# Batch 0 of an attention and gated-MLP kernel: q's product in 64-column tiles, one-pass transposes, twelve unread matmuls left out, another order of all work

## The chip, the cores and the metric

The kernel runs on one core of a Trainium2 chip. The time is device microseconds (us) of one execution. The core has a matrix engine (TensorE, PE in the rows; PEld is its loading of weights), a vector engine (VectorE, DVE), a scalar engine (ScalarE, ACT), GpSimd (POOL), and SyncE (SP), which here issues the DMAs. PE writes to PSUM, which POOL can't reach.

## What is computed

First a linear-time attention with product features, for 4 batches and 4 heads of 32 columns over 1088 positions; then a gated MLP whose gate mixes the positions with a 1088 x 1088 matrix. The reference, cut to that:

```python
def phi(x):
    a = np.einsum('rd,bhsd->bhsr', S1, x)
    b = np.einsum('rd,bhsd->bhsr', S2, x)
    return np.einsum('bhsi,bhsj->bhsij', a, b).reshape(*x.shape[:-1], r * r)   # r = 8
q_p, k_p = phi(q), phi(k)
kv = np.einsum('bhsf,bhsd->bhfd', k_p, v)
z = np.sum(k_p, axis=2)
x = np.einsum('bhsf,bhfd->bhsd', q_p, kv) / (np.einsum('bhsf,bhf->bhs', q_p, z)[..., None] + 1e-06)
...                                            # heads side by side: x is (4, 1088, 128)
h = gelu_tanh(x @ w_in)                        # w_in 128 x 1024
u, v = h[..., :512], h[..., 512:]
v_n = (v - mean(v)) / np.sqrt(var(v) + 1e-06) * g_ln
v_s = np.einsum('ts,bsd->btd', w_sg, v_n) + b_sg[None, :, None]   # w_sg 1088 x 1088
out = x + (u * v_s) @ w_out                    # w_out 512 x 128
```

## The kernel before

Large products are done in fp32r with operands that are split into a high and a low part (names with `_h` and `_l`): high x high, low x high and high x low are added in PSUM. Small products in the head are plain fp32, for which the trace shows two records each. Positions lie in 9 blocks of 128. PSUM has eight banks: `pst` (three, handed out in turn, `ps` in the rows), `pzt` (two, `pz`) and `pot` (three, `po`).

Batch 0's head goes like this. `k1_0` (L531) makes k's factors, `features` (L270) on DVE their products, `k2_0` (L539) the key product in 64-column weight tiles; `kv_0` (L551, L553) cuts it into `kvx`, a block-diagonal operand with a column for the denominator. `q2_0` (L608) makes q's factors in three blocks of 384 positions, ACT copies one of two (L622), DVE multiplies (L623). `q3_0` (L586) is q's product with `kvx`: for each block of 384 positions six matmuls with 128 weight columns and 66 moving ones. `xt_0` (L593 to L595) divides by the denominator on DVE, `tr_0` (L602) transposes with a matmul by the identity, ACT and DVE split x into its two parts (L630, L631). Then the nine gate groups `v1_0` (L636 to L638; 512 columns, one for each block of positions) make v; ACT does the GELU (L653), and batch-norm statistics follow on DVE (L642) or ACT (L655, L656). The norm is done in three groups of blocks (2, 4 and 3 of them) by small operations on DVE or POOL (L299 to L333), then v is scaled (L336, L669) and split into `ar` and `rs` (L676, L677). The mixing product of batch 0 comes next, w's blocks by v's: `z0` (L700, L702, L698 for w's low part) into `po`, and a second one (L1264, L1266, L1262) into `pz`. Beside it the attention of batch 1 begins: `k1` (L947), q's factors (L980), the key product (again L539).

w_in, w_out and S1, S2 come as 64-bit floats and are split by a chain of integer operations on DVE and ACT, `split64` (L473 to L496; its last step L496 makes the low part, `win_l`). w itself is cast to its high part by ACT (L671); the low part `w_l` is made by POOL for the first seven blocks (L718) in pieces of 420, 420 and 248 columns, and by DVE for the last two. Batches 1 to 3 follow with the same kinds of operations (L849 to L851 for most of the mixing).

Every operation is a step of a list with an engine, its dependences and its buffers (`step`, `add`). A table of numbers, `ORDER`, says in which order the steps are recorded; each engine runs its own in that order, and SP issues its DMAs in it. A step that waits holds back all that stands behind it on its engine. The list has also `KEEP = 12` steps `keep`, which multiply a part of `win_h` by another into the first `pz` bank, and which nothing reads. In the head, the DMAs' places in the table were bound by a rule: `first_loads` gives an order, and each load had to come behind the one before it in its row.

Of the kernel before, what the change touches and what calls it, by code (L numbers as in the profile page):

```python
# [34 lines left out]
KEEP = 12  # L35
# [173 lines left out]
def tile_kernel(ctx: ExitStack, tc: tile.TileContext, qd, kd, vd, sd, wd, bd, wind, gd, woutd, identd, outd):  # L209
# [290 lines left out]
    for n, dma, f in first_loads():  # L500
# [3 lines left out]
        if n == "win1":  # L504
            split64("s", None, None, raw_s, 16, s_f, ["s"], ())
            split64("wi1", win_h[:, DG:], win_l[:, DG:], lambda: raw_w("wi1"), DG, None, ["win1"], ())
# [73 lines left out]
    def view(c):  # L580
        return pzt[c % 2][:, : 6 * n2].rearrange("p (g e) -> p g e", e=D + 1)
# [801 lines left out]
```

## Time and profile before

| | us |
|---|---|
| runs: median of 3 (lowest to highest) | 327.1 (326.97 to 327.31) |
| the profiled execution, whole | 327.88 |
| its span, first to last instruction | 326.1 |
| PE busy | 316.9 (97%) |
| DVE busy | 257.4 (79%) |
| ACT busy | 208.5 (64%) |
| POOL busy | 49.8 (15%) |

Rows of the profile give the start of an instruction or of a run of equal ones in us from the span's start, or sums over a group. Matmuls are pipelined, so their records overlap, and what one costs in a row of them is the distance between starts. `[... <-DVE x L1]` behind an instruction means that its engine was idle before it, until that instruction on DVE was done. A chain follows what ended last back to the start, each piece with its length.

### The profile page before, as it was taken

The page shows a single profiled execution, that of the slowest core. Times are in us where ns is not written, and L with a number is a line of the kernel's source. Part 1 is how long each engine was busy: PE and PEld are TensorE (multiplying, and loading weights), DVE is VectorE, ACT ScalarE, POOL GpSimd, SP SyncE. Part 2 cuts the span into 40 slices and gives each one's busy share as a digit, 9 for nine tenths or more (in the row PEclk, how much of TensorE's full clock was granted, in tenths as well). Part 3 has the DMA queues.
Part 4 walks back from the last instruction along what each step waited for, and adds up shares of the span by engine and source line. Part 5 has one row for each costly group of instructions (what it writes and reads, how often), then busy time and mean ns, then how long its engine had stood idle before and what let it go on. Part 6 is the DMA issues. An engine that isn't in the chain of part 4 may idle for free.

```text
span 326.1 us, 6435 instructions
## 1 busy us (share of the span) xinstructions
PE 316.9 (97%) x2303; PEld 287.2 (88%) x2303; DVE 257.4 (79%) x567; ACT 208.5 (64%) x494; POOL 49.8 (15%) x125
## 2 busy tenths in 40 slices
PE   8997999999999999999999999999999999999995
PEld 6764789888888998799899999898999999999994
DVE  4799889999987888787866788996864794878564
ACT  5577795557887993565889855457869952333241
POOL 0197673100004300000005200000013200000000
PEclk9999999999999999999999999999999999999999
DMA  7992875657778857972285239940553035506602
GB/s 222 362 384 68 292 222 173 185 156 155 222 216 264 267 160 222 298 266 61 82 286 171 72 99 251 295 108 3 158 150 143 1 106 178 182 26 210 215 2 69
DMA packets 42128, 57.10 MB, mean 175 GB/s; under 512 B 4208, under 2 KB 37104, under 8 KB 42096
## 3 DMA queue, kind: packets, MB, share of 16 engines
q1 hardware_dynamic: 41952, 56.62, 56.2%
q8 instruction: 18, 0.29, 0.4%
q14 instruction: 14, 0.11, 0.1%
q10 hardware_dynamic: 144, 0.06, 0.1%
HBM read 46.73 MB, written 9.95 MB: 174 GB/s over the span
## 4 chain that ended last, share of the span: by engine, by line
PE 77%; DVE 8%; ACT 7%; DMA 4%; issue 2%; SPq 1%; DVEq 0%; ACTq 0%
PE pz L849 14%; PE pz L850 13%; PE pz L851 13%; PE ps L764 2%; PE pz L860 2%; PE po L801 2%; PE ps L766 2%; PE ps L539 2%; PE ps L765 2%; PE ps L1007 2%; PE po L803 2%; PE po L802 2%; PE pz L861 2%; PE ps L1041 2%; PE po L700 2%
## 5 line engine op out<-in xcount | busy, mean ns | idle before, releaser
L849 PE MATMUL pz<-w_h,ar 128*128 128x420 f32 (+1 forms) x288 | 94.2, 327 | 0.2 <-DVE gt L780 0.2
L850 PE MATMUL pz<-w_h,ar 128*128 128x420 f32 (+1 forms) x288 | 93.2, 324 | 0.0
L851 PE MATMUL pz<-w_l,ar 128*128 128x420 f32 (+1 forms) x288 | 93.1, 323 | 0.0
L849 PEld LDWEIGHTS pz<-w_h,ar 128*128 128x128 f32 x288 | 54.1, 188 | 4.3 <-issue 1.7
L850 PEld LDWEIGHTS pz<-w_h,ar 128*128 128x128 f32 x288 | 54.1, 188 | 1.3 <-DVE ar L825 0.2
L851 PEld LDWEIGHTS pz<-w_l,ar 128*128 128x128 f32 x288 | 54.2, 188 | 0.6
L824 ACT CAST ar<-vn 128x512 fp32r<-128x512 f32 x40 | 24.5, 618 | 27.1 <-PE pz L851 20.2
L795 ACT CAST gh<-gt 128x420 fp32r<-128x420 f32 (+1 forms) x47 | 23.0, 493 | 21.2 <-DVE gt L794 18.5
L770 ACT ACTIVATE u<-ps 128x420 f32<-128x420 f32 (+1 forms) x48 | 22.4, 470 | 13.5 <-PE ps L766 7.3
L825 DVE TENSOR_TENSOR ar<-vn,ar 128x512 fp32r<-128x512 f32 x40 | 27.1, 684 | 3.4 <-ACT ar L824 3.2
L796 DVE TENSOR_TENSOR gl<-gt,gh 128x420 fp32r<-128x420 f32 (+1 forms) x47 | 24.6, 533 | 5.6 <-ACT gh L795 5.4
L794 DVE TENSOR_TENSOR gt<-gt,u 128x420 f32<-128x420 f32 (+1 forms) x47 | 24.9, 532 | 3.6 <-ACT u L770 2.9
L336 ACT ACTIVATE vn<-vn,st 128x512 f32<-128x512 f32 x33 | 25.6, 811 | 0.0
L718 POOL TENSOR_TENSOR w_l<-w_f,w_h 128x420 fp32r<-128x420 f32 (+1 forms) x21 | 22.3, 1085 | 18.5 <-DVE sp_wi_t L474 14.3
L780 DVE SCALAR_TENSOR_TENSOR gt<-pz,g_col,b_bc 128x420 f32<-128x420 f32 (+1 forms) x31 | 17.6, 569 | 3.9 <-PE pz L861 2.8
L1050 ACT ACTIVATE vn<-ps 128x512 f32<-128x512 f32 x27 | 16.0, 593 | 6.0 <-PE ps L1043 6.0
L1053 ACT ACTIVATE kp<-vn,st 128x512 bf16<-128x512 f32 x27 | 19.4, 720 | 0.5
L319 POOL TENSOR_TENSOR st<-st 128x4 f32<-128x4 f32 (+2 forms) x8 | 3.0, 381 | 103.3 <-DVE st L301 103.3
L764 PE MATMUL ps<-x_h,win_h 128*128 128x420 f32 (+1 forms) x48 | 15.8, 330 | 0.2 <-ACT r L1016 0.2
L766 PE MATMUL ps<-x_l,win_h 128*128 128x420 f32 (+1 forms) x48 | 15.7, 328 | 0.0
L765 PE MATMUL ps<-x_h,win_l 128*128 128x420 f32 (+1 forms) x48 | 15.7, 327 | 0.0
L801 PE MATMUL po<-gh,wout_h 128*128 128x420 f32 (+1 forms) x47 | 15.7, 334 | 0.0
(264 smaller groups left out, 722.5 us busy)
## 6 DMA issues: line engine op xcount, KB each, us to landing
w_h<-td SPq DMA_DIRECT2D x26, 420.0 KB
w_l<-td SPq DMA_DIRECT2D x52, 210.0 KB
td<-tmp SPq DMA_DIRECT2D x16, 315.0 KB
w_f<-in_w SPq DMA_DIRECT2D x9, 544.0 KB
eb<-dq SPq DMA_DIRECT2D x6, 364.0 KB
ea<-dq SPq DMA_DIRECT2D x12, 182.0 KB
vn<-in_k SPq DMA_DIRECT2D x3, 576.0 KB
tmp<-in_w SPq DMA_DIRECT2D x8, 210.0 KB
```

The source lines that it names most:

```text
L336: return A.activation(self.vn(t), self.vn(t), AF.Identity, bias=self.nm[:, t : t + 1], scale=self.rs[:, t : t + 1])
L718: return G.tensor_sub(w_l[t][:, cs], w_f[t][:, cs], f32(w_h[:, t, cs]))
L764: mm(o, lhsT=win_h[:, ws], rhs=xh[:, cs], start=True, stop=False)
L770: add("A", 0.02 + ap(cw), lambda: A.activation(utt[plan.got[u]][:, :cw], ps(k)[:, :cw], AF.Gelu_apprx_tanh), r=[k], take={u: "u"}, free=[k ...
L794: add("V", dv(cw), lambda: V.tensor_mul(gt(k)[:, :cw], gt(k)[:, :cw], utt[plan.got[u]][:, :cw]), r=[u], w=[k], free=[u], port=1)
L795: add("A", ac(cw), lambda: A.copy(ght[plan.got[h]][:, :cw], gt(k)[:, :cw]), r=[k], take={h: "gh"})
L796: add("V", dv(cw), lambda: V.tensor_sub(glt[plan.got[l]][:, :cw], gt(k)[:, :cw], f32(ght[plan.got[h]][:, :cw])), r=[h, k], take={l: "gl"}, ...
L824: add("A", ac(n), lambda: A.copy(dst[:, 0], q()), r=r, w=[key])
L825: add("V", dv(n), lambda: V.tensor_sub(dst[:, 1], q(), f32(dst[:, 0])), r=r, w=[key], port=1)
L849: mm(o, lhsT=ar[e][:, 0, t], rhs=wh, start=first, stop=False, skip_group_check=True)
L850: mm(o, lhsT=ar[e][:, 1, t], rhs=wh, start=False, stop=False, skip_group_check=True)
L851: mm(o, lhsT=ar[e][:, 0, t], rhs=wl, start=False, stop=last, skip_group_check=True)
```

## The change

Six things are changed. `q3_0` makes 12 matmuls with 64 weight columns for a block of 384 positions, in place of six with 128, and lays the result out so that the two denominators of a pair of heads stand side by side. The addition of 1e-6 to the denominator goes from DVE to a new ACT step, `xd`. `kv_0` makes `kvx` with two DVE operations in place of four. `tr_0` uses PE's transpose mode, which takes one pass in place of fp32's two records. The 12 `keep` steps are gone. The low part of w_in's second half, `win_l`, is added up by POOL (`G`) and not by DVE. The loads of the head may stand anywhere in `ORDER`, and the whole table is another one, so that steps of all batches stand in other places.

```diff
-KEEP = 12
...
-    1, 11, 12, 13, 14, 15, 16, 17, 18, 42, 49, 2, 3, 4, 46, 47, 48, 0, 52, 43,
+    2, 1, 11, 12, 3, 4, 13, 14, 0, 15, 16, 17, 18, 50, 42, 45, 46, 43, 53, 47,
...
-        row = "w" if n[1:].isdigit() and n[0] == "w" else "raw" if n in ("win0", "win1", "wout") else n if n in "gb" else ""
-        step(("ld", n), "SP", 0.47 * len(dma), f, dma=dma, order=[last[x] for x in {row, ""} if x in last], after=[("wi1", 5), ("wi1", 4)] if n == "wout" else [])
-        ids[n] = last[row] = ids["ld", n]
+        step(("ld", n), "SP", 0.47 * len(dma), f, dma=dma, after=[("wi1", 5), ("wi1", 4)] if n == "wout" else [])
+        ids[n] = ids["ld", n]
...
-            split64("wi1", win_h[:, DG:], win_l[:, DG:], lambda: raw_w("wi1"), DG, None, ["win1"], ())
+            split64("wi1", win_h[:, DG:], win_l[:, DG:], lambda: raw_w("wi1"), DG, None, ["win1"], (), G)
...
     def kv_0():
-        a = pzt[1][:, :P].rearrange("p (a d) -> p a d", a=4)
-        m = mask.rearrange("p (h d) -> p h d", h=2)
+        m = mask.rearrange("p (h d) -> p h d", h=2)[:, :, :1].broadcast_to([P, 2, D + 1])
         for i in range(2):
-            V.tensor_mul(kvx()[:, i, :, :D], a[:, 3 * i].unsqueeze(1).broadcast_to([P, 2, D]), m)
-        for i in range(2):
-            V.tensor_mul(kvx()[:, i, :, D], a[:, i + 1, :1].broadcast_to([P, 2]), m[:, :, 0])
+            a = pzt[1][:, (3 * D - 1) * i :][:, : D + 1]
+            V.tensor_mul(kvx()[:, i], a.unsqueeze(1).broadcast_to([P, 2, D + 1]), m)
...
     def q3_0(c):
         for t in range(3):
             for p in range(2):
-                mm(
-                    pzt[c % 2][:, 2 * n2 * t : 2 * n2 * (t + 1)].rearrange("q (h p e) -> q p h e", h=2, p=2)[:, p],
-                    lhsT=qp0(c, p)[:, P * t : P * t + P], rhs=kvx()[:, p], start=True, stop=True,
-                )
+                o = view(c)[:, 2 * t : 2 * t + 2, (D + 1) * p :][:, :, : D + 1]
+                for e in (0, 64):
+                    mm(o[e : e + 64], lhsT=qp0(c, p)[:, P * t + e : P * t + e + 64], rhs=kvx()[:, p], start=True, stop=True)
+
+    den0 = staged("den", [P, 12], None)
+
+    def xd_0(c):
+        return A.activation(den0(c).rearrange("p (g e) -> p g e", e=2), view(c)[:, :, D : D + 2], AF.Identity, bias=eps_t)
 
     def xt_0(c):
-        den = stage([P, 12], f"den{c}", f"den0_{c}")
-        V.tensor_scalar(den, view(c)[:, :, D], EPS, None, op0=ALU.add)
-        V.reciprocal(den, den)
+        V.reciprocal(den0(c), den0(c))
...
     def tr_0(c):
         for t in range(3):
             cs = slice(P * t, P * t + P)
-            mm(ps(("px0", c))[:, cs], lhsT=xt0[c][:, cs], rhs=ident(), start=True, stop=True)
+            mm(ps(("px0", c))[:, cs], lhsT=xt0[c][:, cs], rhs=ident(), start=t == 0, stop=t == 2, is_transpose=True, skip_group_check=True)
...
-    for i in range(KEEP):
-        step(("keep", i), "PE", 0.233, lambda: mm(pzt[0], lhsT=win_h[:, DG : DG + P], rhs=win_h[:, DG:], start=True, stop=True), [("wi1", "hi")], w=[("psn", 0)])
```

What the new table does to the engines' order is seen in three places. The line numbers below are each kernel's own; in the new kernel they are two to five lower.

The first is DVE behind the features of k, up to the first product of the attention (`r`). L623 (new L620) multiplies q's factors, `sp_wi` are steps of the split of w_in's second half, `den` are denominators. Before:

```order
L623 TENSOR_TENSOR vn<-pz_114,eb 128x384
L623 TENSOR_TENSOR vn<-po_117,ea 128x384
L551 TENSOR_TENSOR sg_kvx<-pz_115,mask 128x2x32 x2
L553 TENSOR_TENSOR sg_kvx<-pz_115,mask 128x2 x2
L623 TENSOR_TENSOR vn<-po_117,eb 128x384
L623 TENSOR_TENSOR vn<-ps_111,ea 128x384
L473 TENSOR_SCALAR sp_wi_t<-sg_wraw_wi_277 128x512
L593 TENSOR_SCALAR den_0_314<-pz_114 128x12
L594 RECIPROCAL den_0_314<-den_0_314 128x12
L595 TENSOR_TENSOR r_101<-pz_114,den_0_314 128x384
```

And now:

```order
L620 TENSOR_TENSOR vn<-po_117,ea 128x384
L620 TENSOR_TENSOR vn<-pz_114,eb 128x384
L471 TENSOR_SCALAR sp_wi_t<-sg_wraw_wi_227 128x512
L472 SCALAR_TENSOR_TENSOR sp_wi_t<-sg_wraw_wi_227,sp_wi_t 128x512
L474 SCALAR_TENSOR_TENSOR sp_wi_t<-sp_wi_m,sp_wi_t 128x512
L477 TENSOR_SCALAR sp_wi_g<-sp_wi_t 128x512
L547 TENSOR_TENSOR sg_kvx<-pz_115,mask 128x66 x2
L620 TENSOR_TENSOR vn<-ps_113,ea 128x384
L620 TENSOR_TENSOR vn<-po_117,eb 128x384
L493 TENSOR_TENSOR sp_wi_t<-sp_wi_t,win_h 128x512
L590 RECIPROCAL sg_den_313<-sg_den_313 128x12
L591 TENSOR_TENSOR r_101<-pz_114,sg_den_313 128x384
```

Four steps of the split went ahead of `kvx`, and a fifth ahead of the first reciprocal.

The second is POOL from its first low part of w on; `w_l_321` (new `w_l_315`) is block 0 of it, `w_l_363` (new `w_l_421`) block 1. Before:

```order
L718 TENSOR_TENSOR w_l_321<-w_f_140,w_h 128x420 x2
L930 MEMSET eb 128x64
L718 TENSOR_TENSOR w_l_321<-w_f_140,w_h 128x248
L718 TENSOR_TENSOR w_l_363<-w_f_141,w_h 128x420 x2
L718 TENSOR_TENSOR w_l_363<-w_f_141,w_h 128x248
```

And now:

```order
L713 TENSOR_TENSOR w_l_315<-w_f_140,w_h 128x420 x2
L713 TENSOR_TENSOR w_l_315<-w_f_140,w_h 128x248
L494 TENSOR_TENSOR win_l<-sp_wi_t,sp_wi_e 128x512
L713 TENSOR_TENSOR w_l_421<-w_f_141,w_h 128x420 x2
L713 TENSOR_TENSOR w_l_421<-w_f_141,w_h 128x248
```

`win_l` came in behind block 0.

The third is PE from the last gate group to the first matmuls of the mixing product; L712 are the `keep` steps, L947 (new L942) and L980 (new L975) belong to batch 1. Before:

```order
L638 MATMUL ps_112<-win_h,x_l 128x512
L712 MATMUL pz_114<-win_h 128x512
L947 MATMUL ps_113<-sk,vn 64x64 x2
L947 MATMUL ps_112<-sk,vn 64x64 x2
L712 MATMUL pz_114<-win_h 128x512 x4
L947 MATMUL ps_111<-sk,vn 64x64 x2
L712 MATMUL pz_114<-win_h 128x512 x4
L947 MATMUL ps_112<-sk,vn 64x64 x2
L947 MATMUL ps_113<-sk,vn 64x64 x2
L700 MATMUL po_116<-w_h,ar_89 128x420
```

And now:

```order
L636 MATMUL ps_111<-win_h,x_l 128x512
L975 MATMUL ps_113<-qld,sk 64x182 x2
L942 MATMUL ps_112<-sk,vn 64x64 x2
L942 MATMUL ps_111<-sk,vn 64x64 x2
L942 MATMUL ps_113<-sk,vn 64x64 x2
L942 MATMUL ps_112<-sk,vn 64x64 x2
L942 MATMUL ps_111<-sk,vn 64x64 x2
L942 MATMUL ps_113<-sk,vn 64x64 x2
L698 MATMUL po_117<-w_h,ar_89 128x420
```

The `keep` steps are out, and batch 1's first matmuls, of which some stood between the gate groups, now all stand behind the last one.

## Rows read from the trace of the kernel before

**Rows 1.** Windows: stretch, length, busy PE, PEld, DVE, ACT, POOL, clock, DMA, GB/s.

```profile
core 0 of [0], span 326.1 us
...
7.00:8.00 1.00, 1.00 (x20) 0.52 (x16) 0.70 (x3) 0.81 (x2) 0.00 (x0) 1.00 1.09 371
...
150.00:200.00 50.00, 50.00 (x409) 46.17 (x408) 36.88 (x79) 36.90 (x92) 6.72 (x24) 1.00 0.45 141
```

**Rows 2.** The chain that ended last, in the head: start, length, what.

```profile
3.05 5.23 DMA sg_vx<-in_v
...
8.32 2.20 PE pz L539 x68
...
16.61 1.01 ACT w_h L671
...
21.30 0.61 ACT vn L653
...
33.81 1.13 PE pz L712 x4
34.94 0.27 PE ps L947 x4
...
36.71 0.39 PE po L700
```

**Rows 3.** PE's weight loads in order of time: start, length, what, count.

```profile
11.94 1.42 PEld L586 LDWEIGHTS pz<-sg_kvx,vn 128*128 128x128 f32 x12 [0.54 <-issue]
...
16.60 1.41 PEld L602 LDWEIGHTS ps<-sg_ident,r 128*128 128x128 f32 x12 [0.55 <-DMA qld<-in_q]
```

**Rows 4.** PE's matmuls in order of time, at the start of the mixing products.

```profile
36.64 0.46 PE L700 MATMUL po<-w_h,ar 128*128 128x420 f32 x1
36.94 0.35 PE L702 MATMUL po<-w_h,ar 128*128 128x420 f32 x1
...
43.28 0.35 PE L1264 MATMUL pz<-w_h,ar 128*128 128x420 f32 x1
```

**Rows 5.** DVE in order of time, in the head.

```profile
17.61 0.55 DVE L623 TENSOR_TENSOR vn<-pz,ea 128x384 f32<-128x384 f32 x1
18.07 0.68 DVE L495 TENSOR_TENSOR sp_wi_t<-sp_wi_t,win_h 128x512 f32<-128x512 f32 x1
18.67 0.68 DVE L480 SCALAR_TENSOR_TENSOR sp_wi_e<-sp_wi_e,sp_wi_g 128x512 f32<-128x512 f32 x1
...
21.05 0.23 DVE L594 RECIPROCAL den<-den 128x12 f32<-128x12 f32 x1
21.32 0.56 DVE L595 TENSOR_TENSOR ea<-pz,den 128x384 f32<-128x384 f32 x1
21.93 0.69 DVE L642 BATCH_NORM_STATS2 st<-vn 128x6 f32<-128x512 f32 x1
...
22.76 0.66 DVE L642 BATCH_NORM_STATS2 st<-vn 128x6 f32<-128x512 f32 x1
...
26.00 1.05 DVE L306 TENSOR_TENSOR st<-st 128x2 f32<-128x2 f32 x1
27.09 0.16 DVE L307 TENSOR_TENSOR st<-st 128x2 f32<-128x2 f32 x1
...
34.95 0.42 DVE L677 TENSOR_TENSOR ar<-vn,ar 128x256 fp32r<-128x256 f32 x1
```

**Rows 6.** The instructions on `win_l`: line, engine, count, ns min/median/max, starts.

```profile
L496 POOL TENSOR_TENSOR win_l<-sp_wi_t,sp_wi_e x1: 1294/1294/1294, 59.5 to 59.5; 128x512 fp32r<-128x512 f32 x1
```

**Rows 7.** POOL in order of time; the second row has pieces of 420 and 248.

```profile
15.30 2.87 POOL L718 TENSOR_TENSOR w_l<-w_f,w_h 128x420 fp32r<-128x420 f32 x2 [14.34 <-DVE sp_wi_t L474]
...
18.83 8.21 POOL L718 TENSOR_TENSOR w_l<-w_f,w_h 128x248 fp32r<-128x248 f32 x8 [0.57 <-DVE sp_wi_t L495]
```

**Rows 8.** Windows, two of PE's emptiest: columns as in rows 1.

```profile
27.00:28.00 1.00, 0.57 (x9) 0.37 (x8) 0.83 (x6) 0.57 (x3) 0.04 (x1) 1.00 0.01 2
...
325.00:326.10 1.10, 0.00 (x0) 0.00 (x0) 0.00 (x0) 0.00 (x0) 0.00 (x0) 0.51 0.00 0
```

**Rows 9.** Groups by line: busy us, mean ns of one, idle before.

```profile
L780 DVE SCALAR_TENSOR_TENSOR gt<-pz,g_col,b_bc 128x420 f32<-128x420 f32 (+1 forms) x31 | 17.6, 569 | 3.9 <-PE pz L861 2.8
```

More of the change, by code (lines that the diff above doesn't have):

```diff
@@ L498, in tile_kernel @@
     step("vx1", "G", 0.1, lambda: G.memset(vx()[:, NT], 1.0))
-    last = {}
     for n, dma, f in first_loads():
-        row = "w" if n[1:].isdigit() and n[0] == "w" else "raw" if n in ("win0", "win1", "wout") else n if n in "gb" else ""
-        step(("ld", n), "SP", 0.47 * len(dma), f, dma=dma, order=[last[x] for x in {row, ""} if x in last], after=[("wi1", 5), ("wi1", 4)] if n == "wout" else [])
-        ids[n] = last[row] = ids["ld", n]
+        step(("ld", n), "SP", 0.47 * len(dma), f, dma=dma, after=[("wi1", 5), ("wi1", 4)] if n == "wout" else [])
+        ids[n] = ids["ld", n]
         if n == "win1":
             split64("s", None, None, raw_s, 16, s_f, ["s"], ())
-            split64("wi1", win_h[:, DG:], win_l[:, DG:], lambda: raw_w("wi1"), DG, None, ["win1"], ())
+            split64("wi1", win_h[:, DG:], win_l[:, DG:], lambda: raw_w("wi1"), DG, None, ["win1"], (), G)
     m4 = mask4.rearrange("q (p h) -> q p h", p=2)
@@ L560, in tile_kernel @@
             ps(("pk0", c))[:, : 3 * 64].rearrange("q (t p x c) -> q t p x c", t=3, p=2, x=2)[:, :, :, 1],
-        ), [pk])
+        ), [pk], r=[pk])
         for i in range(3):
@@ L565, in tile_kernel @@
             step(("kp0", t), "V", 0.34, lambda c=c, i=i, t=t: features(vn[:, t, 512:768], ps(("pk0", c))[:, 64 * i : 64 * i + 64], kb0(c)[:, i]),
-               [("kb0", c)], w=kk, free=[pk] if i == 2 else [])
+               [("kb0", c)], r=[pk], w=kk, free=[pk] if i == 2 else [])
             step(("k2_0", t), "PE", 0.45, lambda t=t: k2_0(t), ["v0", "v1", "vx1"], r=kk + [("vx", 0), ("vx", 1)], w=[("psn", 1)])
     QT = [(("po", 0), ("po", 1)), (("po", 2), ("psn", 0)), None, (("po", 0), ("po", 1)), (("po", 2), ("psn", 0)), None]
-    n2 = 2 * (D + 1)
+    n2 = 2 * (D + 2)
     def pab0(j, i):
@@ L580, in view @@
     def view(c):
-        return pzt[c % 2][:, : 6 * n2].rearrange("p (g e) -> p g e", e=D + 1)
+        return pzt[c % 2][:, : 6 * n2].rearrange("p (g e) -> p g e", e=n2)
     def q3_0(c):
@@ L585, in q3_0 @@
             for p in range(2):
-                mm(
-                    pzt[c % 2][:, 2 * n2 * t : 2 * n2 * (t + 1)].rearrange("q (h p e) -> q p h e", h=2, p=2)[:, p],
-                    lhsT=qp0(c, p)[:, P * t : P * t + P], rhs=kvx()[:, p], start=True, stop=True,
-                )
+                o = view(c)[:, 2 * t : 2 * t + 2, (D + 1) * p :][:, :, : D + 1]
[4 more added lines that the diff above has]
+        return A.activation(den0(c).rearrange("p (g e) -> p g e", e=2), view(c)[:, :, D : D + 2], AF.Identity, bias=eps_t)
     def xt_0(c):
-        den = stage([P, 12], f"den{c}", f"den0_{c}")
-        V.tensor_scalar(den, view(c)[:, :, D], EPS, None, op0=ALU.add)
-        V.reciprocal(den, den)
+        V.reciprocal(den0(c), den0(c))
         V.tensor_tensor(
-            xt0[c].rearrange("p (g d) -> p g d", d=D), view(c)[:, :, :D], den.unsqueeze(2).broadcast_to([P, 12, D]), op=ALU.mult
+            xt0[c].rearrange("p (g e d) -> p g e d", e=2, d=D), view(c).rearrange("p g (e d) -> p g e d", e=2)[:, :, :, :D],
+            den0(c).rearrange("p (g e) -> p g e", e=2).unsqueeze(3).broadcast_to([P, 6, 2, D]), op=ALU.mult
         )
@@ L627, in tile_kernel @@
         step(("q3_0", c), "PE", 1.36, lambda c=c: q3_0(c), ["kv0", ("qp", 2 * c), ("qp", 2 * c + 1)], w=[("psn", c % 2)])
-        step(("xt", c), "V", 0.94, lambda c=c: xt_0(c), [("q3_0", c)] + [("qp", 4)] * (c == 2), r=[("psn", c % 2), "ea"])
+        step(("xd", c), "A", 0.2, lambda c=c: xd_0(c), [("q3_0", c)], r=[("psn", c % 2)])
+        step(("xt", c), "V", 0.8, lambda c=c: xt_0(c), [("q3_0", c), ("xd", c)] + [("qp", 4)] * (c == 2), r=[("psn", c % 2), "ea"])
         step(("tr", c), "PE", 0.68, lambda c=c: tr_0(c), [("xt", c), "ident"], r=["ea"], take={("px0", c): "ps"})
```

185 rows, old and new, of the table ORDER are left out of this document.

## The prediction

> **What bounds the kernel now.** I read the windows first, then the chain of waits, then each engine's timeline for the first 45 us. In the windows TensorE (PE) is busy 50.00 of the 50 us from 150 to 200, and it is nearly like that from 42 to 322 us [rows 1]: there the end is PE's work added up. The head is different. Its chain goes from v's load, which lands at 8.3, over the key product L539 to the first GELU at 21.30; at 33.81 it rests on four L712, matmuls whose result nobody reads, and at 36.71 it comes to the first mixing matmul of batch 0, L700 [rows 2]. PE does fillers there because it has nothing else that it may do. So PE time that is taken out counts only as far as the work that PE waits for comes earlier too, and I cost the change twice: by PE's work, and by when that chain lets PE go.
>
> **PE's work.** The 12 fillers L712 fall away. Four of them stand on the chain with 1.13 us [rows 2], 0.28 each: 12 x 0.28 = 3.4 us. q's product L586 has two records for each fp32 matmul; 12 of them, one third of the batch, take 1.42 us [rows 3], 0.118 apart. It becomes 24 records a third with 64 weight columns. The nearest row is L539, the same width with 64 moving columns for 66: 68 records in 2.20 us, 0.032 apart [rows 2]. 24 x 0.032 = 0.78, so 0.64 is saved in each third, 1.9 in all. At the other bound 64-column weights would keep the old spacing, cost 2.8 a third and lose 4.2 in all; I take the row of the same shape. The nine transposes L602 take 18 records, 12 of them 1.41 us [rows 3]; with one pass each, 9 remain. A one-pass transpose is in no row. Its bounds are a 64-column record's 0.032 and both old records' 0.235; I take 0.118, since one pass is what one record is, and save 9 x 0.118 = 1.1 (1.8 or nothing at the bounds). Together PE loses 3.4 + 1.9 + 1.1 = 6.4 us. Against it stand some two more switches between 64- and 128-column weights: behind such a switch L700 starts at 36.64 and the next matmul 0.30 later instead of 0.19 [rows 4], so 0.2 us for two, which I leave in the range.
>
> L602's records overlap: each lasts 275 ns, and they start 118 ns apart. The Trainium skill ("TensorE: Matmul & The Clock Gate", Part 4: PE-mode transpose) gives about 275 ns for a transpose inside a kernel; by that the nine would cost 2.5 us, PE would lose 5.0 instead of 6.4, and my forecast would be some 0.5 us higher, for three of them on the chain. The trace agrees with that figure as a record's length, and not as what one costs in a row of them.
>
> **The chain through the head, step by step.** Loads: q's second block (192 KB) now goes ahead of v. At 371 GB/s, which the loads reach from 7 to 8 [rows 1], that is 0.5 us, so v lands at 8.8, and L539, with two q products moved ahead of it, ends at about 11.3 for 10.5.
>
> DVE (VectorE) has in its new order four steps of the split of w_in's second half (now ahead of kvx), kvx in two operations, two products of q's features, the split's rest, and for each block a reciprocal and a product. What one takes of DVE is the distance between starts: 0.46 for a 384-wide product, 0.60 for a 512-wide split step, 0.26 for a reciprocal [rows 5]. From 10.4, when the first two products are done: split steps 2.0 (two of them shorter), kvx 0.35, two products 0.9, a wait of 0.3 for ACT's high part, a split step 0.6, reciprocal and product 0.7, a split step 0.6, reciprocal and product 0.7, four more 384-wide operations 1.9. That ends at 18.5, when x's second low part is done. q's product lies beside it on PE, 0.8 us for 1.4.
>
> The low part of w_in's second half, win_l, moves from DVE to GpSimd (POOL). There it takes 1.29 us [rows 6], for 0.6 of DVE's time. It stands behind the three pieces of the first w_l, and these behind ACT's cast of w_h, which now ends at about 13.4; 1.43 for each 420-wide piece [rows 7] and 0.75 for the short one give 17.0, and win_l is there at 18.3. The first gate group needs it, x's low part and q's third product, all between 18.0 and 18.4. Behind the group, the 1.01 us cast that ACT has there and the GELU's place of 0.5 [rows 2], the first GELU is done at 20.0.
>
> From there DVE sets the pace: six batch-norm operations at 0.83 [rows 5] and x's last low part at 0.45 lead to 25.4. Fifteen small operations of the norm follow. One takes 0.2 of DVE when it is alone, and 1.05 when POOL's w_l pieces run beside it [rows 5]. POOL's nine pieces, at 8.21/8 each [rows 7], run from 18.3 to 27.6. So two small operations fill 25.4 to 27.6 and 13 follow: 30.2. A feature product, the scaling, ACT's high part and DVE's low part (0.42 [rows 5]) make 1.8: the first L700 can go at 32.0. Before, that low part was there at 35.37 and L700 went at 36.64. Behind it DVE has 3.5 us of operations up to the second low part and 1.0 more for the next product's, so PE can start L1264 at 36.5. It started at 43.28 before [rows 4].
>
> PE has then done less than it had at 43.28: missing are the key product of batch 1 (72 records x 0.032 = 2.3), two groups of L947 (0.27 each [rows 2]), a q product (0.3) and two pairs of 248-wide L700 (0.5), 3.6 us together. Gain: 43.28 - 36.5 - 3.6 = 3.2 us. Of PE's 6.4 us one half thus turns into waiting, between 25 and 32 above all. Behind the head the engines have the same operations in another order, which I take at nothing; what covers it is that DVE lost about 1.2 us of work and stands as far ahead as PE does.
>
> Span 326.1 - 3.2 = 322.9. The profiled execution took 327.88 and the median of the runs is 327.1, 0.8 lower; the gain put on the median gives **323.9 us**. If none of the small norm operations is slowed the chain is 1.7 us shorter; if four are, 1.7 longer. This case's own range is 322.2 to 325.8.
>
> **The rivals.**
> (a) All of PE's removed work is gained, because the head's chain is shorter than I make it (nothing slows the small operations, and L947 fills the waits): 327.1 - 6.4 = 320.7. For it: PE ends last nearly everywhere [rows 1]. Against it: in my sum DVE has hardly a pause from 10 to 32.
> (b) The clock falls. Between 25 and 32 PE is left with one q product and six groups of L947, 1.9 us of 7. Before, its emptiest us there was 0.57 busy and the granted clock stayed 1.00; it fell to a mean of 0.51 only behind the last matmul, the lower of the two levels (1.2 for 2.4 GHz) [rows 8]. The fillers are part of what kept PE busy in that stretch. At the lower level 2.0 us of L700 would take 4.0, from 32.0 to 36.0, which still ends ahead of L1264 at 36.5; each us of work behind that costs one more. From 0.5 to 3.5 us; with 1.7, 325.6. The Trainium skill ("TensorE: Matmul & The Clock Gate", section HAM oscillation) says that waits between bursts of matmuls bring the half rate back. No row here shows that within the kernel.
> (c) The order behind the head is worse. Place: the two accumulators pz; a new product waits until DVE has evacuated the old one, unless other matmuls stand between. A bare handover costs what the evacuation takes, 0.57 [rows 9]. Before there were hardly any (50.00 of 50 [rows 1]). From seven of them, 4.0 us, the kernel is slower than before: 327.9. Against it: in the new rows other products' matmuls do stand between.
> (d) POOL brings win_l late. If w's first load holds the cast back to 15.8 and the 420-wide pieces take 1.6, it is there at 21.0 instead of 18.4, and every gate group behind it: 2.6 us of the 3.2 are lost, 326.5, no change.
>
> **How the numbers follow.** My forecast 0.47, (a) 0.19, (b) 0.16, (c) 0.09, (d) 0.09. Within 0.2% of 327.1 (326.45 to 327.75) is what a measurement of this kernel can hardly tell from no change: that is (d). Faster 0.82, same 0.09, slower 0.09. A range from 320.6 to 327.0 leaves out the lower part of (a) and most of (c), less than 0.2 together.
>
> **What would show it.** The new profile should have no 512-wide matmul into pz in the head, q's product at about 0.8 us a third, transposes about 0.12 us apart, win_l on POOL done near 18, the first L700 pair near 32, the first L1264 pair near 36.5, and PE idle by some 8 us in the first 40. The forecast is wrong if the norm's small operations end later than 31, if the clock is below 1.00 between 28 and 40, or if PE has gaps behind 42.

## The result, and the profile after

The changed kernel takes 323.88 us (median of 5 runs, 323.06 to 325.47), the kernel before 327.31 beside it (5 runs, 326.97 to 327.74): ratio 0.9901, 95% interval 0.9872 to 0.9931, so 3.4 us faster. The profiled execution is the fastest of the five, 323.06, with a span of 321.3.

The page's first part, then windows, with the columns of rows 1:

```profile
PE 311.0 (97%) x2318; PEld 284.3 (88%) x2318; DVE 255.1 (79%) x561; ACT 208.0 (65%) x497; POOL 50.4 (16%) x126
```

```profile
0.00:40.00 40.00, 34.41 (x407) 26.51 (x408) 32.64 (x101) 32.27 (x79) 23.84 (x49) 0.96 0.78 267
...
44.00:318.10 274.10, 272.63 (x1890) 253.81 (x1888) 218.25 (x456) 171.75 (x412) 22.59 (x75) 1.00 0.56 165
```

```profile
25.00:28.00 3.00, 1.94 (x14) 1.24 (x12) 2.65 (x14) 2.90 (x11) 2.15 (x7) 1.00 0.02 7
28.00:30.00 2.00, 0.79 (x12) 0.51 (x12) 1.83 (x9) 1.97 (x8) 1.59 (x7) 1.00 0.00 0
30.00:32.00 2.00, 1.62 (x12) 1.34 (x12) 1.85 (x8) 2.00 (x8) 0.42 (x4) 0.82 0.53 82
32.00:34.00 2.00, 2.00 (x10) 1.43 (x9) 2.00 (x7) 1.81 (x6) 1.50 (x7) 0.50 0.94 358
34.00:36.00 2.00, 2.00 (x12) 1.96 (x11) 2.00 (x6) 2.00 (x5) 1.67 (x5) 0.83 0.98 322
```

PE is busy 311.0 us where it was 316.9. It is idle for 5.6 us of the first 40, and for 1.5 of the 274 from 44 to its last matmul. New is the clock: between 25 and 30 PE is busy for 2.7 of 5 us, and from 31.3 to 34.7 the granted clock stands at the lower of its two levels, 0.50 (the windows from 30 to 36 give these ends).

PE's weight loads and its matmuls in order of time show the shorter operations, and what the lower level does to the first mixing products:

```profile
12.73 1.73 PEld L582 LDWEIGHTS pz<-sg_kvx,vn 128*64 128x64 f32 x48 [1.04 <-DVE sg_kvx L547]
...
19.86 0.39 PEld L599 LDWEIGHTS ps<-sg_ident,ea 128*128 128x128 f32 x3
```

```profile
30.98 0.48 PE L698 MATMUL po<-w_h,ar 128*128 128x420 f32 x1
31.27 0.54 PE L700 MATMUL po<-w_h,ar 128*128 128x420 f32 x1
31.61 0.55 PE L698 MATMUL po<-w_h,ar 128*128 128x420 f32 x1
31.96 0.55 PE L700 MATMUL po<-w_h,ar 128*128 128x420 f32 x1
...
35.59 0.35 PE L700 MATMUL po<-w_h,ar 128*128 128x420 f32 x1
35.78 0.35 PE L1259 MATMUL pz<-w_h,ar 128*128 128x420 f32 x1
```

48 records of q's product, two blocks, take 1.73 us, 0.036 apart. The three records of a transposed block (0.39 in all, 0.14 each) start about 0.12 apart. The first mixing matmul goes at 30.98, before at 36.64 [rows 4], but the next ones start 0.35 apart instead of 0.19, until 34.6. The first into `pz` goes at 35.78, before at 43.28 [rows 4].

DVE, and then POOL, on the way there:

```profile
25.96 0.39 DVE L297 TENSOR_SCALAR st<-st 128x4 f32<-128x4 f32 x1
...
28.86 0.16 DVE L312 SCALAR_TENSOR_TENSOR st<-st 128x2 f32<-128x2 f32 x1
...
30.59 0.42 DVE L675 TENSOR_TENSOR ar<-vn,ar 128x256 fp32r<-128x256 f32 x1
```

```profile
16.51 1.27 POOL L494 TENSOR_TENSOR win_l<-sp_wi_t,sp_wi_e 128x512 fp32r<-128x512 f32 x1
17.74 3.88 POOL L713 TENSOR_TENSOR w_l<-w_f,w_h 128x420 fp32r<-128x420 f32 x4
...
21.68 4.56 POOL L713 TENSOR_TENSOR w_l<-w_f,w_h 128x420 fp32r<-128x420 f32 x5
```

POOL's pieces of `w_l` now end at 26.24, and of the norm's 15 small operations on DVE only the first (25.96) still runs beside one of them, at 0.39; the others take 0.16 to 0.20, and the last ends at 29.02. Before, four small operations met those pieces, and the slowest of them took 1.05 [rows 5].

### The profile page after: what moved, and what is told of

It reads as the page before. It is cut to its first block, busy times and chain, and to the rows that moved or that the text cites. A ratio compares the mean times of both kernels' runs of the same rounds, so it can differ in the third digit from the quotient of the medians.

```text
span 321.3 us, 6462 instructions
## 1 busy us (share of the span) xinstructions
PE 311.0 (97%) x2318; PEld 284.3 (88%) x2318; DVE 255.1 (79%) x561; ACT 208.0 (65%) x497; POOL 50.4 (16%) x126
## 4 chain that ended last, share of the span: by engine, by line
PE 89%; DVE 7%; issue 1%; ACT 1%; DMA 1%; SPq 0%; DVEq 0%; ACTq 0%
PE pz L844 16%; PE pz L845 15%; PE pz L846 15%; PE po L796 2%; PE ps L759 2%; PE ps L760 2%; PE ps L761 2%; PE po L798 2%; PE ps L1002 2%; PE po L797 2%; PE pz L856 2%; PE pz L855 2%; PE ps L535 2%; PE ps L1036 2%; PE ps L1037 2%; PE ps L1038 2%
## 5 line engine op out<-in xcount | busy, mean ns | idle before, releaser
L775 DVE SCALAR_TENSOR_TENSOR gt<-pz,g_col,b_bc 128x420 f32<-128x420 f32 (+1 forms) x31 | 17.7, 573 | 4.7 <-PE pz L846 2.8
L775 DVE SCALAR_TENSOR_TENSOR gt<-pz,g_col,gt 128x420 f32<-128x420 f32 x12 | 7.8, 648 | 10.8 <-PE pz L856 9.5
```

Source lines behind the costliest of these rows:

```text
L775: return V.scalar_tensor_tensor(o, z()[:, :cw], col[:, db : db + 1], b_bc[:, c0 : c0 + cw] if other is None else gt(other)[:, :cw], op0=AL ...
```

## The experiments

All were timed against the kernel before on their own chip. It took 327.5 beside e1 to e4, 328.1 beside a0, b2, e5 and e6, and 327.9 beside b1, e7, e8 and e10, so the ratio is what compares kernels of different groups. Each ratio has an interval of 0.2 to 0.4% to either side, 0.6 to 1.3 us: what I give for the difference of two experiments is the size of an effect, and its tenths are not shown.

| kernel | median | ratio to before (95%) |
|---|---|---|
| changed | 323.88 | 0.9901 (0.9872 to 0.9931) |
| a0_after, the same again | 324.13 | 0.9877 (0.9843 to 0.9910) |
| e1_fill | 324.26 | 0.9904 (0.9879 to 0.9929) |
| e6_warm | 324.09 | 0.9899 (0.9858 to 0.9940) |
| e5_warm_fill | 323.61 | 0.9862 (0.9830 to 0.9895) |
| e2_win_dve | 326.61 | 0.9969 (0.9950 to 0.9988) |
| e3_q128 | 325.18 | 0.9935 (0.9912 to 0.9959) |
| e4_tr2 | 325.30 | 0.9935 (0.9911 to 0.9959) |
| e8_q128_tr2 | 325.28 | 0.9912 (0.9887 to 0.9936) |
| e10_order_only | 326.70 | 0.9966 (0.9939 to 0.9992) |
| b2_edits | 327.05 | 0.9968 (0.9941 to 0.9995) |
| b1_nokeep | 328.94 | 1.0033 (1.0011 to 1.0055) |
| e7_dve_later | 328.47 | 1.0003 (0.9979 to 1.0026) |

Executions differ from each other at two places of the head (below), so in the profiles I measure from a common mark: x's first low part on DVE (L629), at 17.80 in the changed kernel.

### The clock: a0_after, e1_fill, e6_warm, e5_warm_fill

The theory: PE's waits between 27 and 31 cost the clock, and this costs time. e1_fill puts unread matmuls where PE waits, in the step `k1` of batch 1:

```diff
+                for _ in range({0: 4, 1: 4, 3: 1, 4: 1}.get(c, 0) if b == 1 else 0):
+                    mm(pzt[0], lhsT=win_h[:, DG : DG + P], rhs=win_h[:, DG:], start=True, stop=True)
```

> The changed kernel with 10 unread 512-wide matmuls into pz put back, but only where PE waits: four behind the first group of batch 1's k1 (L942), four behind the second, one behind the fourth, one behind the fifth. My theory: PE's waits between 27 and 31 us make the granted clock fall to 0.50 from about 31.2 to 34.6, and that costs some 1.5 us (a 420-wide matmul starts 0.35 behind the last there, 0.19 elsewhere). Then the clock stays 1.00 here, the first L1259 pair (L1261 in this file) starts near 34.3 instead of 35.8, and the time is about 322.4 against 323.9. Rival 1: DVE's low part at 34.2 and what follows it set the pace, so PE only waits later: clock 1.00, time within 0.4 of 323.9. Rival 2: the fillers stand ahead of groups that could go, each costs 0.1 to 0.3: first L698 later than 31.3, time 324.2 or more. Rival 3: the clock falls for another reason: 0.50 in 31 to 34.6 as before, 323.9.

> The changed kernel, unaltered, as the control for the runs beside it: median 323.9, as before within 0.5. In the profile one of two heads: k's factors (L527, 36 records) in 1.4 us, as in its first profile, or in 2.2 to 2.5 us, as in two of the experiments, and then everything from 7 us on is 1.1 to 1.3 later.

e6_warm has `WARM = 17` for 14, and e5_warm_fill both edits.

> The changed kernel with 17 unread matmuls at the start (L263) in place of 14, so that PE works until about 4.8 us instead of 4.1 and waits 0.2 instead of 0.9 ahead of k's factors. Theory: in part of the executions TensorE runs at its lower level from 5 to 9 us because of that wait (L527's 36 records in 2.5 us, in others 1.36), and those executions are some 1.3 longer; then the longest runs go, the median falls by about 0.5, and the lowest stays at 323.1. Rival: the lower level there does not depend on that wait: median and scatter as in the control. Other rival: the last of these matmuls ends after sk is there (5.0) and holds L527 up: 0.2 longer.

> Both: 17 matmuls at the start, and the 10 fillers between 27 and 32 us of e1_fill. In e1_fill the granted clock stayed 1.00 behind 26 us, and seen from the same point of the head the later products went 0.5 earlier, not 1.5, since DVE's low parts (35.5, 36.6 there) then set the pace. Theory: 0.5 from the fillers and 0.5 from the warm-up, together about 322.9 against the control's 323.9. Rival: fillers are worth nothing (e1_fill's median was 324.3): as e6_warm.

Windows of the control a0_after, and then of e5_warm_fill:

```profile
28.00:30.00 2.00, 0.48 (x10) 0.21 (x6) 1.66 (x11) 1.97 (x8) 1.42 (x7) 1.00 0.02 4
30.00:32.00 2.00, 1.19 (x14) 0.89 (x16) 1.97 (x7) 2.00 (x8) 1.30 (x6) 0.61 0.07 16
32.00:34.00 2.00, 2.00 (x8) 1.38 (x8) 1.93 (x8) 2.00 (x6) 0.65 (x3) 0.50 0.76 173
34.00:36.00 2.00, 2.00 (x11) 1.82 (x11) 2.00 (x7) 1.87 (x7) 1.50 (x6) 0.50 1.00 385
36.00:38.00 2.00, 2.00 (x9) 1.93 (x9) 2.00 (x5) 2.00 (x3) 1.83 (x4) 0.68 0.98 341
```

```profile
28.00:30.00 2.00, 2.00 (x18) 1.22 (x17) 1.81 (x9) 1.97 (x9) 1.50 (x8) 1.00 0.00 0
30.00:32.00 2.00, 1.90 (x15) 1.41 (x14) 1.87 (x8) 2.00 (x8) 0.53 (x4) 1.00 0.49 62
32.00:34.00 2.00, 1.96 (x15) 1.52 (x14) 2.00 (x8) 1.81 (x5) 1.49 (x6) 1.00 0.89 340
```

That the waits cost the clock is shown: from 18 to 42 us it stays at 1.00 in the profiles of all five kernels with the fillers, and falls to 0.50 in all six profiles of the new order without them. (The Trainium skill, "TensorE: Matmul & The Clock Gate", section HAM oscillation, has it so: waits between bursts of matmuls bring the half rate back. These windows agree.) In the control it stays low longer than in the first profile, to about 37.3. The first matmul into `pz` comes 18.0 us behind the mark in the changed kernel, 18.7 in the control, and 17.0 in both filled ones: the lower level costs 1.0 to 1.7 us there, net of what the fillers cost (the first L698 goes 0.2 later with them). Behind batch 1's key product 0.7 to 1.4 of it is left (22.0 and 22.7 against 21.3). With the clock held, PE waits for DVE instead, as rival 1 of e1_fill had it; this is PE in e5_warm_fill:

```profile
33.98 0.35 PE L698 MATMUL po<-w_h,ar 128*128 128x420 f32 x1
34.37 0.46 PE L700 MATMUL po<-w_h,ar 128*128 128x420 f32 x1
...
35.05 0.35 PE L1261 MATMUL pz<-w_h,ar 128*128 128x420 f32 x1
35.43 0.46 PE L1263 MATMUL pz<-w_h,ar 128*128 128x420 f32 x1
```

L700 starts 0.39 behind L698 instead of 0.19, and L1263 likewise: DVE's low parts end at 34.32 and 35.38. In the time of the whole kernel the fillers show less still. e5_warm_fill is 0.5 below the control, and e1_fill no better than the changed kernel. e5_warm_fill's profile gives the gain back behind the head: from the first pair behind batch 1's key product it needs 283.1 us to the end, the control 281.3, with short waits for DVE and a load between 50 and 120. e1_fill's profile doesn't: it needs 281.6, and its span of 322.2 is 0.9 below the control's 323.1, with the mark 0.1 later. The long rests, 282.7 to 283.6, are those of four profiles with 17 starting matmuls (e5, e6, e8, e10); the six with 14 need 281.3 to 282.1. I can't say why. So the lower clock's price in the head is shown, and whether it is a price in the end stays open.

The second place is the start. PE on k's factors and the first key product, in the changed kernel and then in the control:

```profile
5.06 1.36 PE L527 MATMUL ps<-sk,k 128*64 128x64 f32 x36 [0.93 <-DVE sk L506]
...
9.15 2.32 PE L535 MATMUL pz<-sg_vx,vn 128*64 128x64 f32 x72
```

```profile
5.16 2.25 PE L527 MATMUL ps<-sk,k 128*64 128x64 f32 x36 [0.99 <-DVE sk L506]
...
10.81 1.39 PE L535 MATMUL pz<-sg_vx,vn 128*64 128x64 f32 x40
```

The same instructions take 0.9 us longer, the next five L605 2.29 for 1.34, and the head is 1.4 later at the mark. With 14 starting matmuls the key product began between 10.6 and 10.9 in three of six profiles, and by 9.5 in the others; with 17 it began by 9.71 in all five. The medians of e6_warm and its control are equal, with one run of e6_warm at 327, so whether this is worth anything stays open.

### The parts in the new order: e2_win_dve, e3_q128, e4_tr2, e8_q128_tr2, e10_order_only

e2_win_dve gives `win_l` back to DVE:

```diff
-            split64("wi1", win_h[:, DG:], win_l[:, DG:], lambda: raw_w("wi1"), DG, None, ["win1"], (), G)
+            split64("wi1", win_h[:, DG:], win_l[:, DG:], lambda: raw_w("wi1"), DG, None, ["win1"], ())
```

> The changed kernel with win_l back on DVE, at the same place of the table (behind x's two low parts, ahead of the third denominator). My theory: DVE sets the pace from 10 to 29 us, so its 0.6 us shows in full: first GELU near 20.9 instead of 20.3, norm's last small operation near 29.6 instead of 29.0, time about 324.4 against 323.9. Rival: DVE waits 0.6 at 20.4 and 0.2 later, so the 0.6 falls into that wait and the time is within 0.2 of 323.9. A second rival: w's low parts on POOL end 1.27 earlier without win_l, and what waits for them gains.

It costs 2.7 us against the changed kernel by the medians and 2.2 by the ratios, some four times DVE's 0.6. POOL and DVE in e2_win_dve:

```profile
20.71 3.88 POOL L713 TENSOR_TENSOR w_l<-w_f,w_h 128x420 fp32r<-128x420 f32 x4 [3.16 <-ACT sg_den L587]
...
24.64 4.54 POOL L713 TENSOR_TENSOR w_l<-w_f,w_h 128x420 fp32r<-128x420 f32 x5
```

```profile
19.90 0.68 DVE L494 TENSOR_TENSOR win_l<-sp_wi_t,sp_wi_e 128x512 fp32r<-128x512 f32 x1
...
27.66 0.89 DVE L297 TENSOR_SCALAR st<-st 128x4 f32<-128x4 f32 x1
28.58 0.72 DVE L298 TENSOR_SCALAR st<-st 128x4 int32<-128x4 int32 x1
29.34 0.17 DVE L299 TENSOR_SCALAR st<-st 128x4 int32<-128x4 int32 x1
```

The next block of `w_l` waits 3.16 us on POOL and starts 0.13 behind the end of DVE's `win_l` (20.58), though the row names ACT; in e10_order_only it starts 0.13 behind it too. The kernel itself asks for that wait: where it records the steps (`issue`), a POOL step marked `port` is made to wait for the last DVE step so marked ahead of it in the table (`hold`). With `win_l` on DVE that step is `win_l`; with `win_l` on POOL, `win_l` takes up the wait for the split's last DVE step (L478), and the block of `w_l` behind it has none. So the pieces end at 29.18, 10.2 behind the mark (18.96) instead of 8.4, and two small operations of the norm run beside them, at 0.89 and 0.72. The norm begins 0.5 later behind the mark, which is DVE's share, and ends 1.6 later: the larger part is POOL's. `win_l` on DVE without that wait was not run, so what the move is worth by itself stays open.

e3_q128 and e4_tr2 undo one edit of PE's work each, e8_q128_tr2 both on top of e5_warm_fill, and e10_order_only also gives `win_l` back to DVE:

```diff
-                for e in (0, 64):
-                    mm(o[e : e + 64], lhsT=qp0(c, p)[:, P * t + e : P * t + e + 64], rhs=kvx()[:, p], start=True, stop=True)
+                mm(o, lhsT=qp0(c, p)[:, P * t : P * t + P], rhs=kvx()[:, p], start=True, stop=True)
```

```diff
-            mm(ps(("px0", c))[:, cs], lhsT=xt0[c][:, cs], rhs=ident(), start=t == 0, stop=t == 2, is_transpose=True, skip_group_check=True)
+            mm(ps(("px0", c))[:, cs], lhsT=xt0[c][:, cs], rhs=ident(), start=True, stop=True)
```

> The changed kernel with q3_0 back at six matmuls with 128 weight columns for each block (output layout as in the changed one). My theory: 12 records at 0.118 are 1.42 us a third against about 0.9, so 0.5 a third; the third block stands right ahead of the first gate group and delays it by 0.5, the first two are beside DVE's work. First GELU some 0.5 later, time about 324.4 against 323.9. Rival 1: all three thirds count, PE's work is 1.6 us more: 325.5. Rival 2: hidden by DVE, within 0.2 of 323.9.

> The changed kernel with tr_0 as plain fp32 matmuls by the identity again, two records each. My theory: 18 records instead of 9, 0.118 each, so 1.06 us more PE work, of which the first two blocks' 0.7 lie just ahead of q's third product, which waits for DVE, and the third's 0.35 stands between two gate groups; ACT's and DVE's halves of x come up to 0.35 later. Time 0.3 more, 324.2. Rival 1: all 1.06 counts, 325.0. Rival 2: all hidden, within 0.2 of 323.9.

> e5_warm_fill with both edits of PE's work undone: q3_0 with 128 weight columns, fp32 transposes in two records (2.5 to 3.0 us more of PE work). Each of them alone cost 1.3 in the changed kernel, where the granted clock was then 0.50 for 6 us instead of 3.4. If the clock was the reason, the fillers hold it here and only what lies on the chain counts, 0.5 for the third q product and 0.3 for the transposes: 324.4. Rival: PE's work itself counts, 326.2.

> As e8_q128_tr2, and win_l back on DVE: what is left of the change is the new order, the denominator on ACT and kvx in two operations. Theory: win_l on POOL and the new order need each other (e2_win_dve: 2.5 slower, since POOL then waits 3.2 us for DVE to be done with the split's buffers before it can write the next w_l there, and its pieces run beside the norm's small operations), so the order alone is worth little: 326.5 to 327.5, before 327.5. Rival: the order is the gain, and the edits add to it: 325.0 or less.

Alone they cost 1.3 and 1.4 by the medians, 1.1 each by the ratios, and the granted clock in their profiles stayed at 0.50 until about 38. With the clock held, both together cost 1.7 (e8_q128_tr2 over e5_warm_fill; 1.6 by the ratios), between the theory's 0.8 and the rival's 2.6. PE's weight loads in e8_q128_tr2 say why:

```profile
12.92 2.75 PEld L581 LDWEIGHTS pz<-sg_kvx,vn 128*128 128x128 f32 x24 [0.91 <-DVE sg_kvx L547]
...
17.23 1.41 PEld L598 LDWEIGHTS ps<-sg_ident,r 128*128 128x128 f32 x12 [0.54 <-DMA qld<-in_q]
```

The first two blocks of q's product take 1.0 us longer (2.75 for the changed kernel's 1.73), and x's low part comes just that much later, at 19.02 for e5_warm_fill's 18.06. I had them beside DVE's work; in the new order they lie on the chain. `win_l` on DVE, with POOL's wait, costs 1.4 more (e10_order_only over e8_q128_tr2; 1.8 by the ratios), with POOL's second block at 20.92 after a wait of 4.50. What is then left, the new order with fillers, the denominator on ACT and `kvx` in two operations, is 1.2 us below before, inside the 326.5 to 327.5 of the theory.

### Edits in the old order: b2_edits, b1_nokeep

```diff
-        step(("keep", i), "PE", 0.233, lambda: mm(pzt[0], lhsT=win_h[:, DG : DG + P], rhs=win_h[:, DG:], start=True, stop=True), [("wi1", "hi")], w=[("psn", 0)])
+        step(("keep", i), "PE", 0.233, lambda: None, [("wi1", "hi")], w=[("psn", 0)])
```

is b1_nokeep; b2_edits has in addition the 64-column tiles and the one-pass transposes.

> The kernel before with its old order, and three of the edits: the 12 keep matmuls issue nothing, q3_0 in 64-column tiles, one-pass transposes (win_l stays on DVE, kvx and the denominator as before). PE loses 3.4 + 1.9 + 1.1 = 6.4 us of work. My theory: PE only waits more, since the chain over DVE is as it was (first low part at 35.4, second at 41.4): first L700 0.3 to 1.0 earlier than 36.6, time 326.0 to 327.3, unless the clock falls, then up to 1.5 more. Rival: PE's work is what counts everywhere: 327.4 - 6.4 = 321.0. Rival 2: without the fillers the clock falls in 28 to 38 and the kernel is slower than before: 328 or more.

> The kernel before with its old order, and one edit: the 12 keep matmuls issue nothing. PE loses 3.4 us of work that lies where it waits anyway. My theory: the chain over DVE is as it was, so at most the 0.3 us that the first L700 gains (it stood behind four of them) comes out, and the clock falls in 28 to 38 us in part of the executions and takes it back: within 0.8 of before. In b2_edits, where q's product and the transposes were shorter too, the granted clock was 0.50 from 19 to 25 and from 35.8 to 39, and the median 1.0 lower than before. Rival: the fillers are pure cost, 327.4 - 3.4 = 324.0. Rival 2: they earned their place, without them 1 us slower or more.

b2_edits gains 1.0 us of PE's 6: in the old order, with the clock left to fall, the edits alone are worth little. b1_nokeep is 1.0 slower than before, as its rival 2 had it. Windows of b1_nokeep, and one of b2_edits:

```profile
32.00:34.00 2.00, 1.49 (x15) 0.86 (x14) 1.79 (x7) 1.44 (x5) 1.83 (x4) 1.00 0.63 170
34.00:36.00 2.00, 1.32 (x13) 0.94 (x10) 1.90 (x8) 1.75 (x8) 1.23 (x6) 0.76 0.88 228
36.00:38.00 2.00, 2.00 (x7) 1.88 (x7) 1.69 (x8) 1.89 (x8) 1.49 (x8) 0.50 0.95 318
```

```profile
20.00:25.00 5.00, 5.00 (x14) 3.80 (x15) 3.91 (x11) 3.26 (x6) 5.00 (x6) 0.50 1.08 364
```

Without the fillers the clock falls in the mixing products, which begin at 35.55, 1.1 earlier than before, and lose it again: the first into `pz` is at 43.52 for 43.28. That is 0.2 us, and b1_nokeep's profile, that of the fastest of its 12 executions, is only 0.2 longer than before's (326.3 for 326.1). So the profile shows the clock falling, and not where the 1.0 of the medians lies; that the clock is its cause is likely, not shown. In b2_edits it falls under the gate groups, and again from 36 to 39.

### An attempt at a faster kernel: e7_dve_later

```diff
+for x, a in ((568, 188), (569, 568), (570, 569), (571, 570), (572, 571), (574, 190)):
+    ORDER.remove(x)
+    ORDER.insert(ORDER.index(a) + 1, x)
```

> An attempt at a faster version: e5_warm_fill, and six steps of the preparation of w that DVE and ACT do between 31 and 38 us (L897 to L900, L902, L904: 3.2 us of DVE) moved behind the low parts that the mixing products of batch 0 wait for. Theory: with the clock at 1.00 these low parts are what PE waits for (L700 0.2 us at 34.3, the second L1263 0.2 at 35.4, then k's products 0.3 to 1), so the first L1261 pair goes near 34.7 instead of 35.05 and the one behind batch 1's key product near 38.6 instead of 39.4; time 0.5 to 0.8 below e5_warm_fill, 323.0. Rival: the moved 3.2 us of DVE and the transfers behind them come too late further on, and DVE is the one that is waited for from 50 to 120: as e5_warm_fill or slower.

It is 4.9 us slower than e5_warm_fill by the medians, 4.6 by the ratios. In the profiles 4.3 are seen: 1.0 at the mark (19.09 for 18.06), 2.0 from the mark to the first pair behind batch 1's key product, and the rest behind it. ACT, DVE and PE in its profile:

```profile
37.12 0.72 ACT L905 CAST tmp<-tmp 128x630 fp32r<-128x630 f32 x1 [2.06 <-DVE tmp L902]
```

```profile
41.00 0.76 DVE L271 TENSOR_TENSOR vn<-ps,kb 128x256 f32<-128x256 f32 x2 [2.29 <-ACT kb L954]
```

```profile
38.44 0.34 PE L945 MATMUL ps<-sk,vn 128*64 128x64 f32 x4 [0.93 <-DVE vn L271]
```

I had moved ACT's cast of the moved values right behind them, and it still stood ahead of all of ACT's later work: ACT waits 2.06 us for DVE there, what DVE needs from ACT comes late, DVE waits 2.29, and PE waits for both.

## Why the prediction was right, and which steps were not

The time was forecast as 323.9 and came out at 323.88, a gain of 3.4 us by the medians for a forecast 3.2. But in the head two steps were off, and that they cancelled is luck.

- **PE's work** was 6.4 us in the sum. q's product is 0.036 apart, not 0.032, so a third costs 0.87; the 128-column form is 1.38 in e8_q128_tr2, and 0.5 rather than 0.64 is saved a third. The transposes are about 0.12 apart, the value taken. The sum is near 6.0. By an estimate from the about 275 ns that the Trainium skill ("TensorE: Matmul & The Clock Gate", Part 4: PE-mode transpose) gives, the 6.4 would have been 1.4 less; the trace has 272 to 273 ns as the length of most records and not as their distance.
- **The chain up to the norm** was right: L535 ends at 11.5 (11.3 forecast), x's second low part at 18.8 (18.5), `win_l` at 17.8 (18.3), the first GELU at 20.4 (20.0), the six batch-norm operations at 26.0 (25.4). Rival (d), `win_l` late, did not come.
- **The norm's small operations** were mis-sized: 4.8 us from 25.4 to 30.2, with two of them slowed, where they took 3.1 with one slowed. The mechanism was right. But POOL began its nine pieces at 17.7 instead of 18.3 and took 0.94 for each instead of 1.03, so it was done at 26.2 instead of 27.6, while DVE came to the norm 0.6 later than forecast; one operation met a piece, and it took 0.39 instead of the 1.05 that I gave to each of two. The first mixing matmul went at 30.98 instead of 32.0.
- **The clock** was set at nothing in the forecast, and rival (b) was right: between 25 and 30 PE was busy for 2.7 of 5 us, and the clock fell. It took 1.0 to 1.7 us at the first matmul into `pz`, which came at 35.78 (36.5 forecast) in the first profile and at 37.82 in the control, 1.4 of this from the start. The prediction named a clock below 1.00 between 28 and 40 as a sign that would make it wrong; the sign came, and in the first profile the norm, which ended 1.2 earlier, made up for it. For the waits before, my "emptiest us" was misread: PE is busy for 0.51 from 31 to 32, less than the 0.57 that I named, and the clock stayed at 1.00 there too.
- **What becomes of PE's saved time**: one half did turn into waiting, but less in idle time than I said (5.6 us in the first 40, not 8; it was 4.6 before) and more in matmuls at the lower level.
- **The body at nothing** holds: PE's waits from 44 to its last matmul are 1.5 us, 1.9 before, so rival (c) is out. It is no exact zero, though: by the prediction's own sum (43.28, less the first L1259, less 3.6) the head gains 3.9 in the first profile and 1.9 in the control's, and the spans are 4.8 and 3.0 shorter, about a us more in both. Before's single profile is 0.8 above its median, so this may be scatter. From the first pair behind batch 1's key product to the end the profiles of the new order (but e7_dve_later's) need 281.3 to 283.6 us, which hides gains of half a us from the head.
- **Rival (a)**, all 6.4 gained, is out by the result: the ratio's interval allows 2.3 to 4.2 us. b2_edits has nearly the same cut and gains 1.0, though with the clock at the lower level from about 19 to 26 and 36 to 39.

The 3.4 us is a joint result, and its parts are rough. Taken from the changed kernel with the clock held (e5_warm_fill, 4.5 below before by its ratio), q's product and the transposes are worth 1.6 to 1.7, `win_l` on POOL with the wait that it takes away 1.4 to 1.8, and the order with the rest of the edits 1.1 to 1.2. Taken alone in the old order, where the clock falls, the cut in PE's work is worth 1.0, and the `keep` steps' removal by itself costs 1.0.

## What to carry to other kernels

Where PE waits in a stretch, work taken from it gains only as far as the chain of the other engines comes earlier, and if the work was a filler, its removal can cost the clock for the products behind: look at the granted clock of that stretch before and after. When a step goes to another engine, ask which waits go with it, also those that the kernel itself writes, and not only what it costs; when steps are moved on one engine, move those that wait for them on the other engines too.

## What was not expected of the hardware

The row of the granted clock shows 1.00 from 5 to 10 us in the control, while the same 36 records took 2.25 us there and 1.36 in the other execution, and five 384-wide matmuls 2.29 and 1.34: at the start of the program the distance between records tells PE's pace, and that row doesn't. A DVE operation on 128x2 or 128x4 values takes 0.16 to 0.20 us in the norm of the changed kernel, and 0.26 to 1.05 beside one of POOL's subtractions for `w_l` (before, changed kernel and e2_win_dve).
